# Weight blocks in groups of two, first decay rows by products, and a planned lock between VectorE and POOL

## The chip, the core and the metric

The kernel runs on one core of a Trainium2 chip. A core has five engines that run their own instruction streams and meet at semaphores: TensorE (PE in the profile; its weight loads are shown as PEld), VectorE (DVE), ScalarE (ACT), GpSimd (POOL) and SyncE (SP), which here issues the DMAs. The metric is the device time of one execution in microseconds, as the median of several runs.

## The reference

Attention with a forget gate, followed by a two-layer feed-forward net ("MoE" in the names, though there is only one expert). Batch 8, 8 heads, 576 rows, 64 columns per head; the net has 512 inputs and outputs and 2048 hidden columns. The net's two weight matrices come as 64-bit floats.

```python
scores = scale * np.matmul(q, k.transpose(0, 1, 3, 2))
log_f = np.log(np.clip(f, 0.0001, 1.0))
cum = np.cumsum(log_f, axis=-1)
decay = cum[:, :, :, None] - cum[:, :, None, :]
scores = np.where(causal, -1000000000.0, scores + decay)
attn = np.exp(scores - max) / (sum + 1e-09)
out = np.matmul(attn, v)
...
h = x @ w_in
g = np.where(h >= 1, h, np.where(h <= -1, 0.0, (h + 1) ** 2 / 4))
return g @ w_out
```

Here x is the attention's output with the heads side by side: 4608 tokens of 512 columns.

## The kernel before

**Jobs.** The attention is cut into jobs, one for each batch and pair of heads. Batch 0 is cut once more by rows (`CUTS`): jobs 0 to 3 are rows 0 to 255 of its four head pairs, jobs 4 to 7 its rows 256 to 575; job 8 on are whole batches. A job takes its rows in steps of 128 (`r`). For each step `scores` makes the products of q and k in PSUM (L831) and, on POOL, the decay term in SBUF: `sd = ck * nsig + cqs` (L837), then the causal mask (L841). `ck` holds the running sum of the logarithms along the row, the same in all partitions; `cqs` is the same sum for the row itself, one number in each partition. `weights` adds both and takes the row's minimum on DVE (L923), takes the exponential with its row sum on ACT (L927), and the reciprocal on DVE. The first five jobs (`NPE`) turn their probabilities with products on PE against a diagonal (`turn_rows`, L852 and L863), later ones split them into two f16 halves (L941 and L947) and turn them by DMA (L953). `early_values` or `values` multiplies by v; the result is x, in two f16 halves (L902 and L903, or L977 and L978).

**Decay rows.** `decay_sums` computes all running sums on 64 partitions (L442), one for each batch and head, in the tile `early`, and writes them to DRAM as `cum_d` (L445). `load_first_decay` (jobs 0 to 3, L664) and `load_decay` (later jobs, L675) read a row back, spread over 128 partitions.

**Weights.** A weight matrix comes in pieces of 1 MB, two to a block: piece 2i is 256 hidden columns of `w_in`, piece 2i + 1 the same 256 rows of `w_out`. `weight_split` puts an f32 word together from the two 32-bit halves of a double with three DVE instructions of 128x1024 (L495, L498, L501), takes its norm (L505, `from_norms`), and splits it into two f16 halves (L509, and L511 and L512 on POOL or L514 on DVE). There are 16 pieces in 8 blocks. `CONVERT` says how many conversion steps are written into each job's program.

**MoE.** Tokens are taken in chunks of 256, and a unit is one chunk and one block of 256 hidden columns. `moe_front` makes 24 products for h (L1012), the nonlinearity on ACT and DVE (L1021 to L1023), and g in two f16 halves (L1025 and L1026); `moe_back` adds 12 products to the chunk's output in PSUM (L1041). The scale factors come from `moe_scales`, fifteen small DVE instructions on one to eight columns (L579 to L604). The first two chunks run before all blocks are converted: `EARLY` lists their units in groups, and a group's units have their own scales and their own sum in PSUM, which is copied to the output tile (L1058) or added to it (L1054). A group's scales are written once its last block is converted.

**Order.** The code writes one program. Then `plan` sets every engine's order anew: `traced` finds what depends on what and gives every instruction a rank, its place in the program plus a shift from the table `SHIFT`; `Step.cost` estimates its duration; `arranged` plays the program through, always taking what can begin first, by rank where several can. The orders found are pinned by dependencies without semaphores. All DMAs go through SP in that order. Within an engine nothing overtakes.

Of the kernel before, what the change touches and what calls it, by code (L numbers as in the profile page):

```python
# [91 lines left out]
class Step:  # L92


    def __init__(self, k, ins):
# [22 lines left out]
    def cost(self):  # L118
# [13 lines left out]
        if e == "ACT":  # L132
            return 150 + (0.82 if wide and wide[0][0][:2] in ("s_", "ph", "po") else 0.93) * n + 100 * min(len(self.reads) - 1 + len(self.writes) - 1, 3)
# [187 lines left out]
def kernel(  # L321
# [247 lines left out]

    @of_kind  # L570
    def moe_scales(b, first=0, last=NB - 1, early_group=False):
# [5 lines left out]
        w = early_z[:, :, blocks] if early_group else tiny.tile([P, 5, NB], F32, name="z")  # L577
        z.t, z.h, z.u, z.r, z.o = (w[:, i] for i in range(5))
        nc.vector.tensor_scalar(out=z.t, in0=sw[:, 0, blocks], scalar1=sv[:, b:b + 1], scalar2=None, op0=ALU.mult)  # L579
        nc.vector.tensor_scalar(  # L580
# [641 lines left out]
```

## Time and profile before

| what | value |
|---|---|
| median of three runs | 1062.35 us (1059.92 to 1063.02) |
| the profiled execution | 1060.71 us, span in the trace 1058.9 us |
| TensorE's mean granted clock | 0.973 |
| DMA ck<-cum_d, issue to landing | 4.0 us (median), 288 KB |
| DMA place<-in_moe_w_in_dram, issue to landing | 6.9 us (median), 1024 KB |

The profile is that of one execution. The span runs from the first to the last record; the profiled execution's own time is 1.8 us longer. A group of instructions is named by line, engine and operation, with the tiles written and read, the count, then busy time and mean duration in ns, then the idle time of the engine before them and what ended it. In the timeline the columns are start, duration, engine, line, operation and tiles; a bracket holds the idle time before and who ended it. The table by stretches gives the busy time of each engine in a part of the span, the granted clock (1.00 is full speed), the DMA engines' share and GB/s.

### The profile page before, as it was taken

How to read it: one execution, taken by the hardware profiler on the slowest of the kernel's cores; microseconds unless marked ns; L12 is line 12 of the kernel's file. 1: busy time of each engine (PE TensorE's matmuls, PEld its weight loads, DVE VectorE, ACT ScalarE, POOL GpSimd, SP SyncE). 2: the span in 40 equal slices, each digit the busy share in tenths (PEclk: the TensorE clock that was granted, in tenths of full speed). 3: DMA queues.
4: the chain of work that ended last, by engine and by line, in shares of the span. 5: the costliest groups of instructions: out<-in, count | busy, mean ns of one | idle time of the engine just before them, and what ended most of it. 6: DMA issues, size and time to landing. Idle time of an engine off the chain costs nothing.

```text
span 1058.9 us, 24420 instructions
## 1 busy us (share of the span) xinstructions
PE 1003.1 (95%) x8859; PEld 657.7 (62%) x8859; DVE 793.0 (75%) x2095; ACT 786.9 (74%) x1634; POOL 435.4 (41%) x677
## 2 busy tenths in 40 slices
PE   3769888799999999999999999999999999999998
PEld 2546555366666676667666666666666666677665
DVE  5999999999998878977776677887788866322222
ACT  3788888788888878886776688888888877344443
POOL 2887776736443544442332344454445441000000
PEclk9869899889999999999999999999999999999999
DMA  9967669789997777785455476767676654000000
GB/s 298 305 203 206 167 163 194 182 169 187 198 189 184 175 167 151 170 185 128 119 128 131 81 175 144 158 150 160 147 161 143 142 104 95 3 22 19 3 20 20
DMA packets 406041, 152.18 MB, mean 144 GB/s; under 512 B 379680, under 2 KB 382752, under 8 KB 405920
## 3 DMA queue, kind: packets, MB, share of 16 engines
q1 hardware_dynamic: 405920, 150.62, 61.0%
q8 instruction: 69, 1.13, 0.5%
q14 instruction: 52, 0.43, 0.1%
HBM read 75.64 MB, written 9.58 MB: 80 GB/s over the span
## 4 chain that ended last, share of the span: by engine, by line
PE 56%; DMA 0%; DVE 0%; issue 0%; ACT 0%; DVEq 0%
PE ph L1012 25%; PE po L1041 24%; PE s L831 4%; PE s L968 3%; DMA vst<-in_v_dram 0%; DVE pr L947 0%; PE ph L409 0%; DVE u L1023 0%; PE ph L401 0%; DVE x L978 0%; ACT ot L1058 0%; PE ph L397 0%; ACT u L1022 0%; DVE sdr L923 0%; DVE rc L938 0%
## 5 line engine op out<-in xcount | busy, mean ns | idle before, releaser
L1012 PE MATMUL ph<-x,place 128*128 128x256 f16 (+3 forms) x4608 | 413.1, 247 | 1.2 <-DVE u L1023 0.7
L1041 PE MATMUL po<-place,g 128*128 128x512 f16 x1728 | 403.5, 381 | 2.3 <-ACT g L1025 1.0
L1012 PEld LDWEIGHTS <-place 128*128 128x128 f16 x4608 | 353.2, 99 | 61.9 <-issue 21.3
L1041 PEld LDWEIGHTS <-g 128*128 128x128 f16 x1728 | 165.9, 98 | 180.6 <-issue 8.0
L837 POOL TENSOR_SCALAR sdr<-ck,nsig,cqs 128x128 f32<-128x128 f32 (+1 forms) x192 | 150.1, 789 | 269.3 <-DVE pr L947 258.1
L1023 DVE SCALAR_TENSOR_TENSOR u<-ph,z,u 128x512 f32<-128x512 f32 x128 | 95.6, 747 | 128.5 <-ACT u L1022 128.3
L1021 ACT ACTIVATE u<-ph,z 128x512 f32<-128x512 f32 x128 | 98.8, 772 | 117.3 <-PE ph L1012 116.9
L927 ACT ACTIVATE sdr<-sdr,nm 128x384 f32<-128x384 f32 (+1 forms) x248 | 137.3, 555 | 24.7 <-DVE nm L923 22.2
L947 DVE SCALAR_TENSOR_TENSOR pr<-sdr,rc,pr 128x384 f16<-128x384 f32 (+2 forms) x232 | 126.7, 584 | 8.0 <-ACT pr L941 6.6
L1025 ACT ACTIVATE g<-u,z 128x512 f16<-128x512 f32 x128 | 91.8, 717 | 51.7 <-DVE u L1023 50.9
L1026 DVE SCALAR_TENSOR_TENSOR g<-u,z,g 128x512 f16<-128x512 f32 x128 | 98.2, 767 | 41.0 <-ACT g L1025 40.5
L941 ACT ACTIVATE pr<-sdr,rc 128x384 f16<-128x384 f32 (+1 forms) x236 | 118.7, 556 | 7.3 <-issue 2.8
L831 PE MATMUL s<-qkT 64*64 64x512 f16 (+11 forms) x1056 | 111.4, 336 | 6.0 <-DVE nm L923 2.9
L923 DVE CUSTOM_DVE_ANT_0 sdr<-s,sdr,nalpha 128x128 f32<-128x128 f32 (+1 forms) x192 | 99.0, 544 | 13.1 <-PE s L831 7.4
L841 POOL TENSOR_SCALAR_AFFINE_SELECT sdr<-sdr 128x128 f32<-128x128 f32 x248 | 97.7, 414 | 2.3
L837 POOL TENSOR_SCALAR sd<-ck,nsig,cqs 64x576 f32<-64x576 f32 x48 | 51.1, 1064 | 115.1 <-DMA ck<-cum_d 46.7
L1022 ACT ACTIVATE u<-u 128x512 f32<-128x512 f32 x144 | 89.7, 623 | 1.9
L968 PE MATMUL s<-pT,vs 128*64 128x320 f16 (+3 forms) x1098 | 69.8, 279 | 3.2 <-DVE nm L923 3.2
L968 PEld LDWEIGHTS <-vs 128*64 128x64 f16 x1098 | 48.6, 110 | 27.0 <-issue 9.3
L831 PEld LDWEIGHTS <-qkT 64*128 64x128 f16 (+1 forms) x864 | 32.4, 98 | 44.0 <-issue 29.4
L747 DVE SCALAR_TENSOR_TENSOR qs<-qk,sc,qs 128x640 f16<-128x640 f32 x48 | 45.6, 962 | 5.3 <-ACT qs L745 4.4
L837 POOL TENSOR_SCALAR sdr<-ck,cq 128x384 f32<-128x384 f32 (+3 forms) x48 | 40.4, 842 | 17.1 <-DVE pr L947 12.6
(157 smaller groups left out, 1027.7 us busy)
## 6 DMA issues: line engine op xcount, KB each, us to landing
ck<-cum_d SPq DMA_DIRECT2D x64, 288.0 KB, 4.0
out_dram<-ot SPq DMA_DIRECT2D x36, 256.0 KB, 2.2
qk<-in_k_dram SPq DMA_DIRECT2D x68, 128.0 KB, 2.7
vst<-in_v_dram SPq DMA_DIRECT2D x28, 288.0 KB, 3.4
v<-in_v_dram SPq DMA_DIRECT2D x62, 128.0 KB, 2.8
qk<-in_q_dram SPq DMA_DIRECT2D x60, 128.0 KB, 2.9
place<-in_moe_w_in_dram SPq DMA_DIRECT2D x6, 1024.0 KB, 6.9
place<-in_moe_w_out_dram SPq DMA_DIRECT2D x5, 1024.0 KB, 7.8
```

Of the source, the lines that this page charges most:

```text
L831: nc.tensor.matmul(sds[h % len(sds)][1][p0:p1, c0:c1], lhsT=a[rows, q0 - w.s0:q0 - w.s0 + p1 - p0], rhs=b[rows, c0:c1], start=(i == 0), st ...
L837: nc.gpsimd.tensor_scalar(out=sd[p0:p1, 0:wid], in0=w.ck[h][p0:p1, 0:wid], scalar1=w.nsig if w.p < NQK else w.nsig[p0:p1], scalar2=w.cqs[p ...
L841: nc.gpsimd.affine_select(sd[p0:p1, q0:wid], sd[p0:p1, q0:wid], pattern=[[-1, wid - q0]], channel_multiplier=1, base=0, compare_op=ALU.is_ ...
L923: nc.vector.tensor_tensor_reduce(out=a, in0=sp[:, 0:wid], in1=a, scale=w.nalpha, scalar=BIG, op0=ALU.add, op1=ALU.min, accum_out=nm[:, i:i ...
L927: nc.scalar.activation(a, a, AF.Exp, bias=nm[:, i:i + 1], scale=-1.0, accum_out=sm[:, i:i + 1])
L941: nc.scalar.activation(pr[:, :, 0, i, :], a, AF.Copy, scale=rc[:, i:i + 1])
L947: nc.vector.scalar_tensor_tensor(out=pr[:, :, 1, i, :], in0=a, scalar=rc[:, i:i + 1], in1=pr[:, :, 0, i, :], op0=ALU.mult, op1=ALU.subtract,)
L968: nc.tensor.matmul(av[64 * h:64 * h + 64, at + s0:at + s1], lhsT=w.vs[:, vl, h, t, :], rhs=w.pT[:, t, pl, h, s0:s1], start=(t == 0 and pi ...
L1012: nc.tensor.matmul(ph[:, fi, a0:a1], lhsT=wi[fb][:, wl, t, fi * P:(fi + 1) * P], rhs=xs[b][:, t, xl, s0:s0 + a1 - a0], start=(fi == 0 and ...
L1021: nc.scalar.activation(u, h, AF.Relu, scale=z.u[:, i:i + 1], bias=z.h[:, i:i + 1])
L1026: nc.vector.scalar_tensor_tensor(out=g[:, 1], in0=u, scalar=z.r[:, i:i + 1], in1=g[:, 0], op0=ALU.mult, op1=ALU.subtract)
L1041: nc.tensor.matmul(po[ch][i], lhsT=g[:, gl, fi * TC + i * P:fi * TC + (i + 1) * P], rhs=wo[fb][:, wl, fi, :], start=(first and fi == 0 and ...
```

## The change

**Groups.** `EARLY` gets more and smaller groups, and chunk 1 fewer and larger ones. `FIRST = {4: 2}` puts the values of job 3 in front of job 4's first step, and lets two MoE units follow as soon as they are ready. `CONVERT` has one conversion step in each of jobs 0 to 3 (before: none in job 0, two in job 3). `moe_scales` computes the part that belongs to a block (`block_scales`) once only, for blocks that have none yet, since groups now overlap; each group keeps `r` and `osc` of its own.

**Decay rows of jobs 0 and 1** (`NROW = 2`). Instead of reading back `cum_d`, POOL spreads a column of the identity over 128 columns (`picks`), and PE multiplies it with the running sums: each partition of the product is the picked row. It stands in PSUM, in a tile named `po1`, and as POOL doesn't read PSUM here, ACT makes `sd` of it with one activation (scale `nsig`, bias `cqs`). The mask stays on POOL. Jobs 2 and 3 are as before.

**The plan.** `arranged` gets a lock: a DVE instruction that counts as sharing (a `TensorScalarPtr` or `TensorTensor` of more than one column whose first operand isn't one of the PSUM tiles) and any POOL instruction exclude each other. The later of the two is taken to begin near the other's end, and an instruction that would have to wait is passed over for one that can begin sooner. The cost estimates of DVE, ACT and POOL get new constants, and `SHIFT` other entries.

```diff
+NROW = 2
-EARLY = ((0, 0, 4), (0, 4, 6), (1, 0, 4), (1, 4, 6), (0, 6, 8), (1, 6, 8))
-
-CONVERT = {1: 1, 2: 1, 3: 2, 5: 1, 6: 1, 9: 1, 10: 2}
+EARLY = ((0, 0, 2), (0, 2, 4), (0, 4, 6), (1, 0, 6), (0, 6, 8), (1, 6, 8))
+FIRST = {4: 2}
+
+CONVERT = {0: 1, 1: 1, 2: 1, 3: 1, 5: 1, 6: 1, 9: 1, 10: 2}
...
-SLOW = 1.03
+SLOW = 1.02
+AWARE = True
 LOOK = 50
 SHIFT = {
+    ("across", "DVE"): -800,
+    ("decay_sums", "SP"): -100,
+    ("first_values", "SP"): 200,
+    ("from_norms", "DVE"): -800,
     ("from_norms", "PE"): -100,
-    ("measure", "DVE"): 400,
-    ("moe_back", "DVE"): 200,
-    ("moe_back", "SP"): 800,
+    ("join_scales", "DVE"): 200,
+    ("moe_back", "DVE"): -100,
+    ("moe_front", "DVE"): 400,
+    ("prepare", "ACT"): 1500,
+    ("prepare", "DVE"): -800,
     ("split_values", "ACT"): 1500,
-    ("turn_rows", "ACT"): -25,
-    ("value_max", "DVE"): -100,
-    ("weight_split", "DVE"): 200,
-    ("weights", "POOL"): 400,
+    ("values", "DVE"): 25,
+    ("weights", "POOL"): 200,
 }
...
+        self.shares = (
+            self.engine == "DVE" and ins.opcode in ("TensorScalarPtr", "TensorTensor")
+            and self.writes[0][4] > 1 and self.reads[0][0][:2] not in ("s_", "ph", "po")
+        )
...
         if e == "POOL":
             if self.ins.opcode == "TensorTensor":
-                return 450 + 2.0 * n
-            return 260 + 0.95 * n if "Affine" in self.ins.opcode else 460 + 1.15 * n
+                return 185 + 1.89 * n
+            return 177 + 0.86 * n if "Affine" in self.ins.opcode else 322 + 0.83 * n
...
-        return 170 + 55 * (scalars > 0) + (0.6 if fast else 1.08) * n + (20 if len(self.writes) > 1 else 0)
+        return 147 + 62 * (scalars > 0) + (0.52 if fast else 1.04) * n
...
                     begin = max(t, free[e])
+                    if AWARE and s.shares:
+                        begin = max(begin, pool - 140)
+                    elif AWARE and e == "POOL":
+                        begin = max(begin, hold - 100)
...
             end = t + s.time
+            if e == "POOL":
+                if hold > t:
+                    end = max(end, hold + s.time - 100)
+                pool = end
+            elif s.shares:
+                if pool > t:
+                    end = max(end, pool + max(s.time - 140, 24))
+                hold = end
             free[e] = end - OVERLAP[e]
...
+        if early_group:
+            at = groups.index((first, last + 1))
+            z.t, z.h, z.u = (early_z[:, i * NB + first:i * NB + first + n] for i in range(3))
+            z.r = early_r[:, starts[at]:starts[at] + n]
+            z.osc = early_r[:, starts[-1] + at:starts[-1] + at + 1]
+            fresh = slice(made[0], last + 1)
+            if made[0] <= last:
+                block_scales(*(early_z[:, i * NB + made[0]:i * NB + last + 1] for i in range(3)), b, fresh)
+                made[0] = last + 1
...
     def load_first_decay(w):
         bh = w.b * H + 2 * w.hp
+        if w.p < NROW:
+            pt = ps1.tile([P, DM], F32, name="po1").rearrange("p (h s) -> p h s", h=2)
+            for h in range(2):
+                nc.gpsimd.tensor_copy(picks[h], ident[0:B * H, bh + h:bh + h + 1].broadcast_to([B * H, P]))
+                nc.tensor.matmul(
+                    pt[:, h], lhsT=picks[h], rhs=early[0:B * H, 2 * S:2 * S + w.s1], start=True, stop=True
+                )
+            w.ck += [pt[:, 0], pt[:, 1]]
+            picks[0:2] = []
+            return
...
-            nc.gpsimd.tensor_scalar(
-                out=sd[p0:p1, 0:wid], in0=w.ck[h][p0:p1, 0:wid], scalar1=w.nsig if w.p < NQK else w.nsig[p0:p1],
-                scalar2=w.cqs[p0:p1, r, h:h + 1], op0=ALU.mult, op1=ALU.add,
-            )
+            if w.p < NROW:
+                nc.scalar.activation(
+                    sd[:, 0:wid], w.ck[h][:, 0:wid], AF.Identity, scale=w.nsig, bias=w.cqs[:, r, h:h + 1]
+                )
+            else:
+                nc.gpsimd.tensor_scalar(
+                    out=sd[p0:p1, 0:wid], in0=w.ck[h][p0:p1, 0:wid], scalar1=w.nsig if w.p < NQK else w.nsig[p0:p1],
+                    scalar2=w.cqs[p0:p1, r, h:h + 1], op0=ALU.mult, op1=ALU.add,
+                )
...
-            steps.insert(4 if len(steps) == NT5 else 2, finish)
+            steps.insert(0 if p in FIRST else 4 if len(steps) == NT5 else 2, finish)
...
-        quota = -(-ready() // (NPAIR - (p + NPAIR - 1) % NPAIR))
+        quota = FIRST.get(p) or -(-ready() // (NPAIR - (p + NPAIR - 1) % NPAIR))
```

`picks` are four slices of a tile of the ring named `u`, 64 partitions by 128 columns each. `block_scales` holds the six instructions of `moe_scales` that stood at L579 to L588.

More of the change, by code (lines that the diff above doesn't have):

```diff
@@ L132, in cost @@
         if e == "ACT":
[L133 removed]
+            return 190 + 0.845 * n + 92 * min(len(self.reads) - 1 + len(self.writes) - 1, 3)
         if e == "POOL":
             if self.ins.opcode == "TensorTensor":
[L136 to L137 removed]
+                return 185 + 1.89 * n
+            return 177 + 0.86 * n if "Affine" in self.ins.opcode else 322 + 0.83 * n
         if wide:
@@ L226, in arranged @@
     chains = {e: [] for e in LATE}
+    hold = pool = 0
     fly, dma, warm, border, busy, form = [], 0.0, False, WINDOW, 0.0, None
@@ L457, in decay_sums @@
         )
+    picks = two.tile([P, 2 * TC], F32, name="u")
+    picks = [picks[0:B * H, P * i:P * i + P] for i in range(2 * NROW)]
     place = const.tile([P, 2 * NB + 1, 2, 2 * DM], F16, name="place")
@@ L563, in value_scale, with block_scales @@
         scale_of(sv[:, b:b + 1], pv[:, b:b + 1], m)
-    early_z = const.tile([P, 5, NB], F32, name="early_z")
+    groups = sorted({e[1:] for e in EARLY})
+    starts = [sum(e - f for f, e in groups[:i]) for i in range(len(groups) + 1)]
+    early_z = const.tile([P, 3 * NB + starts[-1] + len(groups)], F32, name="early_z")
+    early_r = early_z[:, 3 * NB:]
+    made = [0]
     class Scales:
         pass
+    def block_scales(t, h, u, b, blocks):
+        nc.vector.tensor_scalar(out=t, in0=sw[:, 0, blocks], scalar1=sv[:, b:b + 1], scalar2=None, op0=ALU.mult)
+        nc.vector.tensor_scalar(
+            out=h.bitcast(I32), in0=t.bitcast(I32), scalar1=1, scalar2=None, op0=ALU.logical_shift_right
+        )
+        nc.vector.tensor_scalar(
+            out=h.bitcast(I32), in0=h.bitcast(I32), scalar1=HALF_BIAS, scalar2=None, op0=ALU.add
+        )
+        nc.vector.reciprocal(u, h)
+        nc.vector.tensor_scalar(out=u, in0=u, scalar1=0.5, scalar2=None, op0=ALU.mult)
+        nc.vector.tensor_scalar(out=h, in0=h, scalar1=0.5, scalar2=None, op0=ALU.mult)
     @of_kind
@@ L576, in moe_scales @@
         n = last + 1 - first
[L577 to L580, printed above, removed]
-            out=z.h.bitcast(I32), in0=z.t.bitcast(I32), scalar1=1, scalar2=None, op0=ALU.logical_shift_right
-        )
-        nc.vector.tensor_scalar(
-            out=z.h.bitcast(I32), in0=z.h.bitcast(I32), scalar1=HALF_BIAS, scalar2=None, op0=ALU.add
-        )
-        nc.vector.reciprocal(z.u, z.h)
-        nc.vector.tensor_scalar(out=z.u, in0=z.u, scalar1=0.5, scalar2=None, op0=ALU.mult)
-        nc.vector.tensor_scalar(out=z.h, in0=z.h, scalar1=0.5, scalar2=None, op0=ALU.mult)
+        if early_group:
[8 more added lines that the diff above has]
+        else:
+            w = tiny.tile([P, 5, NB], F32, name="z")
+            z.t, z.h, z.u, z.r = (w[:, i] for i in range(4))
+            z.osc = w[:, 4, 0:1]
+            block_scales(z.t, z.h, z.u, b, blocks)
         gm = tiny.tile([P, 1], F32, name="gm", bufs=2)
@@ L1072 @@
     units += [(ch, fb) for ch in range(NCH) if ch not in [e[0] for e in EARLY] for fb in range(NB)]
-    groups = sorted({e[1:] for e in EARLY})
     done = 0
@@ L1180 @@
                 converted += 1
-            while ready() and done - before < quota * (i + 1) // len(steps):
+            while ready() and done - before < (quota if p in FIRST else quota * (i + 1) // len(steps)):
                 if units[done] not in bsc and nw < 2 * NB:
```

5 lines of the change are left out of this document (3 added, 2 removed).

## The prediction

> **What bounds the kernel now.** I read the page's first part first, then the same busy times cut into stretches, then the waits of TensorE in the first 100 us, then the instructions around them in order of time.
>
> ```profile
> PE 1003.1 (95%) x8859; PEld 657.7 (62%) x8859; DVE 793.0 (75%) x2095; ACT 786.9 (74%) x1634; POOL 435.4 (41%) x677
> ```
> ```profile
> 0.00:9.00 9.00, 1.97 (x16) 1.60 (x16) 3.17 (x4) 2.56 (x3) 2.45 (x13) 1.00 0.73 218
> 9.00:23.00 14.00, 7.17 (x40) 4.83 (x40) 9.95 (x22) 2.81 (x4) 2.43 (x5) 1.00 0.98 324
> 23.00:54.00 31.00, 20.38 (x128) 15.06 (x128) 26.89 (x72) 23.80 (x68) 25.45 (x36) 0.83 0.99 316
> 54.00:86.00 32.00, 22.53 (x98) 15.00 (x98) 29.34 (x61) 25.39 (x52) 27.57 (x26) 0.68 0.73 232
> 86.00:110.00 24.00, 23.66 (x184) 14.56 (x183) 23.54 (x50) 21.72 (x41) 17.56 (x20) 1.00 0.64 155
> 110.00:231.00 121.00, 103.84 (x718) 59.81 (x719) 114.52 (x322) 102.67 (x216) 82.30 (x111) 0.90 0.77 177
> 231.00:1059.00 828.00, 823.52 (x7680) 546.82 (x7678) 585.59 (x1570) 608.00 (x1254) 277.67 (x468) 1.00 0.57 125
> ```
>
> Each row has the stretch, its length, the busy time of PE, PEld, DVE, ACT and POOL, the granted clock, the DMA share and GB/s. After 231 us PE is idle for 828 - 823.52 = 4.5 us and has the full clock: there PE is the bound, and a faster DVE, ACT or POOL gives at most those 4.5 us. Before 231 us PE is busy 1.97 + 7.17 + 20.38 + 22.53 + 23.66 + 103.84 = 179.6 us, so it idles 51.4 us; and busy time times what the clock lacks (20.38 x 0.17 + 22.53 x 0.32 + 103.84 x 0.10) is another 21 us at a lower clock, an estimate from these means. **The front, 0 to 231 us, holds all that can be won.** Who ends the waits there? DVE is busy 71% from 9 to 23, 87% from 23 to 54, 92% from 54 to 86, 98% and 95% after. From about 54 us on DVE is the bound of the front: it carries attention, MoE and the conversion of the weights at once. Before that there is a gap with another cause:
>
> ```profile
> PE ph L863 <- ACT pr L852: 22.7, 8, 9.5
> ```
> ```profile
> 12.12 2.73 SPq L664 DMA_DIRECT2D ot<-cum_d  x3
> 15.48 0.69 DVE L495 TENSOR_SCALAR qs<-place 128x1024 int32<-128x1024 int32 x1 [1.42 <-DMA place<-in_moe_w_in_dram]
> 20.31 1.92 POOL L837 TENSOR_SCALAR sdr<-ot,cq 128x128 f32<-128x128 f32 x2 [17.24 <-DMA ot<-cum_d]
> 22.63 0.29 DVE L923 CUSTOM_DVE_ANT_0 sdr<-s,sdr 128x128 f32<-128x128 f32 x1 [0.63 <-POOL sdr L841]
> 25.47 0.17 DVE L930 TENSOR_SCALAR rc<-sm 128x2 f32<-128x2 f32 x1 [2.30 <-ACT sdr L927]
> 26.39 1.22 PE L863 MATMUL ph<-pr,sdr 128*128 128x128 f32 x4 [9.47 <-ACT pr L852]
> ```
>
> The chain of the first job is to be read here: the decay rows go out to DRAM and back (issued from 12.12), POOL can use them at 20.31, DVE's row minimum follows at 22.63, PE's first turning of probabilities at 26.39. One of PE's eight waits for L852 is that one, 9.5 us.
>
> **The change, part by part.** First, the decay rows of jobs 0 and 1. Removed: two DMAs of 256 KB out of four (their share of the SP queue too), and half of POOL's decay instructions of jobs 0 to 3. Added: four copies on POOL, four products on PE, eight activations on ACT.
>
> ```profile
> L837 POOL TENSOR_SCALAR sdr<-ot,cq 128x128 f32<-128x128 f32 (+1 forms) x8 | 7.5, 942 | 17.9 <-DMA ot<-cum_d 17.2
> L837 POOL TENSOR_SCALAR pr<-ot,cq 128x128 f32<-128x128 f32 (+1 forms) x8 | 5.3, 668 | 1.2 <-ACT sdr L927 0.5
> L927 ACT ACTIVATE sdr<-sdr,nm 128x128 f32<-128x128 f32 x4 | 1.6, 398 | 0.4 <-DVE nm L923 0.4
> L863 PE MATMUL ph<-pr,sdr 128*128 128x128 f32 x24 | 6.2, 424 | 15.2 <-ACT pr L852 15.2
> L923 DVE CUSTOM_DVE_ANT_0 sdr<-s,sdr 128x256 f32<-128x256 f32 x12 | 4.8, 409 | 0.0
> L923 DVE CUSTOM_DVE_ANT_0 sdr<-s,sdr 128x128 f32<-128x128 f32 x12 | 3.2, 285 | 1.4 <-PE s L831 0.8 <-POOL sdr L841 0.6
> ```
>
> POOL loses (7.5 + 5.3) / 2 = 6.4 us of work in the stretch where it is busy 25.45 of 31 us. The four products have 256 columns where the nearest row, L863, has 128, so 4 x 2 x 0.424 = 3.4 us of PE between 9 and 23, where PE is idle for 6.8 us: nothing. Should that cover go, they cost their 3.4 us. ACT's eight cost about 8 x 0.45 = 3.6 us (0.40 for 128 columns, some 0.1 more for 256) between 9 and 23, where ACT is busy 2.81 of 14 us: nothing there, and 3.6 us if they land after 23. The four copies on POOL are not in the trace; POOL sits idle 17.24 us before 20.31, which hides anything up to that.
>
> The running sums exist when the DMA out is issued, at 9 us; two products, two activations, POOL's mask and DVE's minimum can then follow by about 13 us instead of 22.63. What is late next: the weights, which come at 15.48 in any case, and DVE. So the gain isn't those 9 us but only what DVE can do in its holes. From 9 to 54 DVE is idle 4.05 + 4.11 = 8.2 us. What becomes ready for them is the DVE work of jobs 0 and 1, per job 2 x 0.285 + 2 x 0.409 = 1.4 us of minima and about as much of small scalings and the split of x, together 5.6 us. I take **-4.5 us**; bounds: 0, if the weights set the pace (the DMA share is 0.98 and 0.99 here, so DMA is nearly full), and -8.2, all holes filled. The two DMAs removed are 0.5 MB at 324 GB/s, 1.6 us earlier for the weights behind them; that lies inside these bounds.
>
> Second, groups of two blocks. The first unit can begin with two blocks converted instead of four.
>
> ```profile
> 68.97 0.14 DVE L591 TENSOR_REDUCE gm<-mp 128x1 f32<-128x4 f32 x1
> 71.85 2.26 DVE L603 TENSOR_SCALAR early_z<-early_z 128x4 f32<-128x4 f32 x1
> 74.14 0.18 DVE L604 RECIPROCAL early_z<-early_z 128x4 f32<-128x4 f32 x1
> 75.47 0.47 DVE L903 SCALAR_TENSOR_TENSOR x<-po,sv,x 128x256 f16<-128x256 f32 x1
> ```
> ```profile
> L1012 PE MATMUL ph<-x,place x528: 192/272/421, 85.7 to 263.0; 128*128 128x256 f16 x128, 128*128 128x64 f16 x24, 128*128 128x192 f16 x24
> ```
>
> The group's scales are done at 74.3, x of chunk 0 at 75.9, and PE begins MoE at 85.7. So the scales of four blocks were not late before x: what a smaller group can gain is that its scales and splits leave the DVE queue in front of x. It gains PE work for a stretch (54 to 86) in which PE idles 9.5 us and has a clock of 0.68. But DVE is the bound there, and a unit brings DVE work along. I take **-2.5 us**; bounds 0 and -7.2 (22.53 x 0.32, if the clock is full there). It costs scales: five groups instead of three. A group has nine instructions of its own and six for new blocks, which fall due four times instead of three: 2 x 9 + 6 = 24 more on DVE, at 0.14 us (the row of L591) **+3.4 us**. Upper bound: the fifteen instructions from 68.97 to 74.32 took 5.35 us, so 24 / 15 x 5.35 = 8.6 us; lower: 24 x 0.1 = 2.4, since neighbours overlap. The sums into the output tile stay equal in number: chunk 0 adds three times and chunk 1 once, before it was twice and twice. The conversion moved one job earlier meets weights that land when they land, so I put it at nothing.
>
> Third, the lock. Some DVE instructions last far longer than their like in the same trace, and the longest lie under a POOL instruction:
>
> ```profile
> 71.95 2.12 POOL L512 TENSOR_TENSOR place<-place 128x1024 f16<-128x1024 f32 x1
> ```
> ```profile
> L603 DVE TENSOR_SCALAR early_z<-early_z x3: 222/229/2257, 71.8 to 219.1; 128x2 f32<-128x2 f32 x2, 128x4 f32<-128x4 f32 x1
> L1026 DVE SCALAR_TENSOR_TENSOR g<-u,early_z,g 128x512 f16<-128x512 f32 x16 | 17.6, 1098 | 0.3 <-ACT g L1025 0.2
> L1026 DVE SCALAR_TENSOR_TENSOR g<-u,z,g 128x512 f16<-128x512 f32 x98 | 75.6, 771 | 18.1 <-ACT g L1025 17.6
> L935 DVE TENSOR_SCALAR rc<-sm 128x2 f32<-128x2 f32 x29 | 8.1, 280 | 1.5 <-ACT sdr L927 1.5
> L935 DVE TENSOR_SCALAR rc<-sm 128x2 f32<-128x2 f32 x89 | 16.3, 183 | 11.9 <-ACT sdr L927 11.4
> L514 DVE SCALAR_TENSOR_TENSOR place<-place,sw 128x1024 f16<-128x1024 f32 x5 | 8.1, 1611 | 0.8 <-ACT place L509 0.8
> L514 DVE SCALAR_TENSOR_TENSOR place<-x,sw,place 128x1024 f16<-128x1024 f32 x3 | 3.8, 1265 | 0.0
> ```
>
> L603 on 128x4 took 2.26 us, from 71.85 to 74.11, and POOL's L512 ran from 71.95 to 74.07; its like took 0.22. In the front (first row of each pair) against later or unhurt ones: 16 x (1.098 - 0.771) = 5.2 us, 29 x (0.280 - 0.183) = 2.8, 5 x (1.611 - 1.265) = 1.7, and 2.0 for that one L603: 11.7 us of DVE time in four groups, most of it where DVE is the bound. A plan that sees the lock can put a minimum (it reads PSUM, and its 285 and 409 ns rows show no such tail) under a POOL instruction. It can't do so always, since DVE is over 90% busy with mostly instructions of the hurt kind, so I take under half: **-5 us**. Bounds: -11.7, and +4 where the plan holds back an engine that then idles (a third of the same sum, in the other direction).
>
> The Trainium skill, page "SBUF — State Buffer", section "Who interferes with whom", says that two SBUF inputs, or a two-port mode, on DVE contend with GpSimd, and that "Issue order, not op shape, decides who blocks." The L603 row agrees. That last sentence speaks against this part: a plan fixes the order on each engine and not the moment of issue between two engines; by it this term would be 0 and the sum -3.6 us.
>
> The new constants and the shifted ranks reorder everything; no row prices them. After 231 us they can win 4.5 us at most; I put them at 0.
>
> **Sum:** -4.5 - 2.5 + 3.4 - 5 = -8.6 us. Against the profiled execution (1060.7 us, span 1058.9) that is 1052.1; the median of the three runs, 1062.35, lies 1.6 us above it, so the forecast is 1053.8 us.
>
> **The rivals.** (a) **More comes off.** DVE's holes all fill (-8.2), the lock falls by two thirds (-8), the clock of 54 to 86 recovers mostly (-5), scales +3.4: -17.8, 1044.6 us. For it: PE waits 22.7 us for L852 alone before 100 us. Against: DVE is busy 92% and more from 54 us on, and all this must pass through it.
>
> (b) **Nothing comes of it.** The weights set the pace before 54 us, so the earlier decay rows turn into a wait for weights (-1.6, the DMA time removed); the run's own issue order undoes the planned lock (0); an earlier first unit (-2) pays for its scales (+3.4): 0, 1062 us. For it: a DMA share of 0.98 to 0.99 from 9 to 54. This is also the case that the change doesn't do what it says. The Trainium skill's sentence on issue order, above, would make this case.
>
> (c) **Slower: the early units get ahead of the conversion.** Two units of chunk 0 are due in job 4's first step, with their scales; on DVE they come before the conversion of blocks 4 to 7 and the minima of the long rows.
>
> ```profile
> L1023 DVE SCALAR_TENSOR_TENSOR u<-ph,early_z,u 128x512 f32<-128x512 f32 x16 | 11.9, 741 | 1.3 <-ACT u L1022 1.3
> ```
>
> Price: 2 x (0.741 + 1.098) = 3.7 us of units that come too early, scales at their hurt price 8.6, less 4.5 and 1.6 from the decay rows: +6 us, 1068.5 us. It decides from the moment that DVE has no hole left (54 us on), and only if the last conversion ends later than now. For it: DVE's 92 to 98%. Against: PE's idle 9.5 us there, which the same units fill, and a unit gives PE 12 + 24 matmuls for two DVE instructions.
>
> **How the numbers follow.** A measurement of this kernel tells a change of about 0.3%, 3.2 us. Forecast 0.42 (1047 to 1059), (a) 0.20 (1037 to 1047), (b) 0.17 (1059 to 1065.5), (c) 0.21 (1065.5 to 1072). Faster: 0.42 + 0.20 = 0.62; same 0.17; slower 0.21. The range 1040 to 1068 leaves out the outer third of (a) and about half of (c), under 0.2 together; the bounds of the unknown terms (0 to -8.2, 0 to -7.2, +2.4 to +8.6, +4 to -11.7) reach somewhat farther than that only if all end on one side. The forecast's own range is 1047 to 1059.
>
> **What would show it.** Decay rows: the first L923 (row minimum) before 15 us, PE's first probability turning before 19, and DVE busier than 9.95 of 14 us from 9 to 23. Groups: MoE's first matmul well before 85.7, a granted clock above 0.68 between 54 and 86, five groups of scales. Lock: L1026 in the front near 0.8 us instead of 1.10, L935 near 0.2. Sum: PE idle before its steady part some 43 us instead of 51.4, with no new idle time after. I am wrong if DVE's busy time in the front stays as it is with the lock's tails in other groups, if the last group's scales come later than now, or if PE gets gaps after 231 us, where it has 4.5 us of them today.

## The result, and the profile after

| | before | after |
|---|---|---|
| median | 1061.68 us (1059.92 to 1063.02, four runs) | 1076.18 us (1073.85 to 1080.60, four runs) |
| ratio | | **1.0147** [1.0131, 1.0164] |
| the profiled execution | 1060.71 us, span 1058.9 | 1080.60 us, span 1078.8 |

The change makes the kernel 14.5 us slower; 8 us less was forecast, and the time lies outside the range. The profiled execution of after is its longest of four, 4.4 us above the median, so its stretches hold a little more than the difference of the medians. In the table of experiments the median of before on two of the chips still contains one slow run, which makes the differences there 0.15 (c1, c2, e4, e5) and 0.3 us (a40, a60, p40, p75) smaller; the ratios leave it out.

The page's first part, and then the table by stretches of after (columns as in the prediction):

```profile
PE 1016.5 (94%) x8867; PEld 668.6 (62%) x8867; DVE 770.4 (71%) x2119; ACT 794.7 (74%) x1642; POOL 419.8 (39%) x673
```
```profile
0.00:9.00 9.00, 4.79 (x30) 4.00 (x32) 3.90 (x6) 2.63 (x4) 3.62 (x17) 1.00 0.73 228
9.00:23.00 14.00, 12.20 (x49) 7.98 (x47) 8.74 (x29) 10.02 (x28) 2.64 (x8) 1.00 1.06 383
23.00:54.00 31.00, 20.11 (x106) 15.14 (x107) 27.43 (x79) 22.15 (x51) 22.98 (x24) 0.79 0.78 224
54.00:86.00 32.00, 27.62 (x151) 18.60 (x150) 24.23 (x56) 24.33 (x50) 20.82 (x23) 0.77 0.94 277
86.00:110.00 24.00, 14.96 (x102) 9.11 (x104) 20.79 (x48) 19.43 (x40) 16.70 (x21) 0.92 0.62 138
110.00:231.00 121.00, 101.69 (x680) 58.81 (x678) 108.54 (x325) 96.70 (x204) 74.36 (x106) 0.89 0.80 178
231.00:1079.00 848.00, 835.11 (x7761) 554.98 (x7761) 576.79 (x1582) 619.41 (x1269) 278.67 (x476) 1.00 0.60 122
```

Read it against the same table of before. Up to 86 us PE is busy 64.7 us where it was 52.1: the early gain is there. It is lost again at once: from 86 to 110 PE falls from 23.66 to 14.96. Over the whole front, 0 to 231 us, PE is busy 181.4 us (before 179.6), but 4.3 us of that are the new products (below), so the front has done no more for the rest than before; of the records of MoE's two product lines (L1071 and L1100, before L1012 and L1041) it holds 444 where it held 463. After 231 us there are 20 us more (848 against 828): 11.6 us more of busy PE (work left over by the front, and some 3 us, by estimate, of a lower clock: 0.99 from 265 to 600 us, where before has 1.00), and idle time up from 4.5 to 12.9 us.

DVE is the opposite of what its share suggests. Its busy time in the front fell from 207.4 to 193.6 us, by 13.8 us, and its idle time rose by the same amount. What it waits for now, by the view of waits of DVE, 0 to 231 us (total, times, longest):

```profile
DVE sdr L982 <- PE s L885: 12.7, 5, 4.0
DVE m L570 <- DMA vst<-in_v_dram: 5.0, 5, 1.7
...
DVE pr L982 <- PE s L885: 3.2, 2, 2.9
```

and in before, same view:

```profile
DVE sdr L923 <- PE s L831: 1.9, 4, 0.9
...
DVE m L544 <- DMA vst<-in_v_dram: 0.4, 1, 0.4
```

**The freed DVE time became DVE waiting for PE and for a DMA.** PE, in turn, waits for DVE. The waits of PE over the whole of after:

```profile
PE s L885 <- DVE nm L982: 12.5, 9, 4.3
PE s L768 <- DVE x L1037: 7.5, 2, 4.6
PE ph L433 <- ACT pT L933: 6.3, 1, 6.3
PE ph L433 <- ACT place L531: 6.0, 3, 4.2
...
PE ph L922 <- ACT pr L911: 1.9, 2, 1.6
```

The 22.7 us for L852 in before (L911 is its line in after) are down to 1.9; others stand in their place. I read this, two engines that wait for each other in turn with neither busy, as an order that does not fit. One such place can be followed in the timeline of after, on SP, DVE and PE:

```profile
255.62 0.43 SPq L563 DMA_DIRECT2D vst<-in_v_dram  x1
```
```profile
258.49 0.08 DVE L982 DVE_READ_ACCUMULATOR2_ANT nm<- 128x1 f32 x1
262.66 0.75 DVE L570 TENSOR_REDUCE m<-vst 128x1 f32<-128x576 f32 x1 [4.09 <-DMA vst<-in_v_dram]
263.33 0.88 DVE L849 SCALAR_TENSOR_TENSOR vs<-v,sv,vs 128x640 f16<-128x640 f32 x1
264.13 0.48 DVE L982 CUSTOM_DVE_ANT_0 sdr<-s,sdr,nalpha 128x256 f32<-128x256 f32 x1
...
266.73 0.08 DVE L982 DVE_READ_ACCUMULATOR2_ANT nm<- 128x1 f32 x1
```
```profile
266.86 0.61 PE L885 MATMUL s<-qkT 64*128 64x512 f16 x2 [4.29 <-DVE nm L982]
```

L570 takes the maximum of a later batch's values. The plan put it at the head of DVE's queue at 258.5 us, but its data had been asked for only at 255.62 and came at 262.6. Two row minima (L982, at 264.13 and 266.32) stood behind it in DVE's queue; the second was done at 266.8, and for it PE waited 4.29 us, in the stretch where PE is the bound. That is about half of the 8.4 us of new PE gaps after 231 us.

### The profile page after: what moved, and what is told of

Same layout as the page of the kernel before. It is cut to its first block, busy times and chain, and to the rows that moved or that the text cites. A ratio compares the mean times of both kernels' runs of the same rounds, so it can differ in the third digit from the quotient of the medians.

```text
span 1078.8 us, 24463 instructions
## 1 busy us (share of the span) xinstructions
PE 1016.5 (94%) x8867; PEld 668.6 (62%) x8867; DVE 770.4 (71%) x2119; ACT 794.7 (74%) x1642; POOL 419.8 (39%) x673
## 4 chain that ended last, share of the span: by engine, by line
PE 66%; DVE 6%; DMA 3%; SPq 3%; issue 2%; ACT 1%; POOL 0%; DVEq 0%; POOLq 0%
PE ph L1071 28%; PE po L1100 28%; PE s L885 5%; PE s L1027 4%; DMA vst<-in_v_dram 3%; DVE sdr L982 1%; DVE pr L1006 1%; SPq L696 1%; DVE qs L801 1%; SPq L841 1%; SPq L700 0%; DVE m L570 0%; DVE g L1085 0%; SPq L806 0%; DMA ck<-cum_d 0%
## 5 line engine op out<-in xcount | busy, mean ns | idle before, releaser
L1071 PE MATMUL ph<-x,place 128*128 128x256 f16 (+3 forms) x4608 | 412.1, 247 | 0.0
L1100 PE MATMUL po<-place,g 128*128 128x512 f16 x1728 | 404.9, 382 | 3.4 <-DVE g L1085 3.0
L1071 PEld LDWEIGHTS <-place 128*128 128x128 f16 x4608 | 354.3, 99 | 61.4 <-issue 20.2
L1100 PEld LDWEIGHTS <-g 128*128 128x128 f16 x1728 | 167.2, 99 | 180.2 <-issue 7.3
L896 POOL TENSOR_SCALAR sdr<-ck,nsig,cqs 128x128 f32<-128x128 f32 (+1 forms) x192 | 139.8, 732 | 250.4 <-DVE pr L1006 216.7
L1006 DVE SCALAR_TENSOR_TENSOR pr<-sdr,rc,pr 128x384 f16<-128x384 f32 (+2 forms) x232 | 131.2, 590 | 25.4 <-ACT pr L1000 24.0
L885 PE MATMUL s<-qkT 64*64 64x512 f16 (+11 forms) x1056 | 116.3, 334 | 16.2 <-DVE nm L982 12.5
L1085 DVE SCALAR_TENSOR_TENSOR g<-u,z,g 128x512 f16<-128x512 f32 x128 | 96.8, 757 | 36.1 <-ACT g L1084 35.8
L900 POOL TENSOR_SCALAR_AFFINE_SELECT sdr<-sdr 128x128 f32<-128x128 f32 x248 | 106.2, 440 | 14.1 <-ACT sdr L892 5.2
L982 DVE CUSTOM_DVE_ANT_0 sdr<-s,sdr,nalpha 128x128 f32<-128x128 f32 (+1 forms) x192 | 98.5, 544 | 16.3 <-PE s L885 12.6
L896 POOL TENSOR_SCALAR sd<-ck,nsig,cqs 64x576 f32<-64x576 f32 x48 | 48.1, 1002 | 138.4 <-DMA ck<-cum_d 45.4
L1027 PE MATMUL s<-pT,vs 128*64 128x320 f16 (+3 forms) x1098 | 72.4, 286 | 5.4 <-DMA qk<-in_k_dram 3.5
L1027 PEld LDWEIGHTS <-vs 128*64 128x64 f16 x1098 | 51.2, 113 | 28.8 <-issue 9.3
L986 ACT ACTIVATION_READ_ACCUMULATOR sdr<-sdr,nm 128x1 f32 x248 | 46.5, 188 | 0.0
```

What stands on the lines that cost most here:

```text
L885: nc.tensor.matmul(sds[h % len(sds)][1][p0:p1, c0:c1], lhsT=a[rows, q0 - w.s0:q0 - w.s0 + p1 - p0], rhs=b[rows, c0:c1], start=(i == 0), st ...
L896: nc.gpsimd.tensor_scalar(out=sd[p0:p1, 0:wid], in0=w.ck[h][p0:p1, 0:wid], scalar1=w.nsig if w.p < NQK else w.nsig[p0:p1], scalar2=w.cqs[p ...
L900: nc.gpsimd.affine_select(sd[p0:p1, q0:wid], sd[p0:p1, q0:wid], pattern=[[-1, wid - q0]], channel_multiplier=1, base=0, compare_op=ALU.is_ ...
L982: nc.vector.tensor_tensor_reduce(out=a, in0=sp[:, 0:wid], in1=a, scale=w.nalpha, scalar=BIG, op0=ALU.add, op1=ALU.min, accum_out=nm[:, i:i ...
L986: nc.scalar.activation(a, a, AF.Exp, bias=nm[:, i:i + 1], scale=-1.0, accum_out=sm[:, i:i + 1])
L1006: nc.vector.scalar_tensor_tensor(out=pr[:, :, 1, i, :], in0=a, scalar=rc[:, i:i + 1], in1=pr[:, :, 0, i, :], op0=ALU.mult, op1=ALU.subtract,)
```

## The experiments

Three theories. **PLAN**: the new constants, shifts and lock make a worse order. **UNITS**: rival (c), early units and their scales push back the conversion. **RESHUFFLE**: any new order costs some us, whatever the change does, because before's order fits better than those near it. The change splits into three parts: groups (`EARLY`, `FIRST`, `CONVERT`), decay rows (`NROW`) and plan (lock, constants, `SHIFT`). "Last scales" is the start of the last group's reciprocal in the profile, a mark for the end of the conversion; it is 220.9 us in before and 227.3 in after. Differences are to the median of before on the same chip.

| run | what it is | median, us | ratio to before | us | last scales |
|---|---|---|---|---|---|
| e1_old_plan | groups + rows, before's plan | 1068.74 | 1.0080 [1.0064, 1.0097] | +8.7 | 229.8 |
| e2_new_plan_only | before + new plan | 1077.94 | 1.0170 [1.0155, 1.0185] | +17.9 | 226.0 |
| e3_rows_only | before + rows | 1071.72 | 1.0109 [1.0094, 1.0124] | +11.7 | 225.6 |
| e4_groups_only | before + groups | 1080.11 | 1.0185 [1.0168, 1.0202] | +19.1 | 231.5 |
| e5_old_shift | after, `SHIFT` of before | 1084.98 | 1.0225 [1.0209, 1.0242] | +23.9 | 238.5 |
| e6_no_lock | after without the lock | 1101.49 | 1.0391 [1.0373, 1.0409] | +41.4 | 240.1 |
| c1_look60 | before, `LOOK` 60 | 1068.76 | 1.0073 [1.0054, 1.0091] | +7.7 | 222.4 |
| c2_look40 | before, `LOOK` 40 | 1068.49 | 1.0073 [1.0057, 1.0089] | +7.4 | 226.3 |
| a40_after_look | after, `LOOK` 40 | 1088.51 | 1.0248 [1.0220, 1.0275] | +28.0 | 235.7 |
| a60_after_look | after, `LOOK` 60 | 1085.82 | 1.0231 [1.0208, 1.0254] | +25.3 | 231.7 |
| e2b_look60 | e2, `LOOK` 60 | 1072.89 | 1.0120 [1.0101, 1.0138] | +12.2 | 225.0 |
| p40_rows_kept | rows, first 40 us planned anew | 1060.16 | 1.0008 [0.9993, 1.0023] | -0.3 | 220.6 |
| p75_rows_kept | rows, first 75 us planned anew | 1065.16 | 1.0044 [1.0027, 1.0061] | +4.7 | 224.9 |
| d1_delay_conversion | before's order, DVE work added in front | 1064.56 | 1.0036 [1.0021, 1.0051] | +3.7 | 224.9 |
| d2_delay_later | before's order, DVE work added later | 1063.22 | 1.0023 [1.0014, 1.0033] | +2.4 | 219.3 |
| l1_no_pool_split | before's order, less POOL work | 1054.40 | 0.9942 [0.9923, 0.9960] | -6.3 | 214.5 |
| g1_first_off | after, `FIRST` empty | 1082.05 | 1.0203 [1.0188, 1.0218] | +21.2 | 232.4 |
| g2_convert_early | after, last conversions earlier | 1089.24 | 1.0272 [1.0254, 1.0289] | +28.4 | 206.7 |

**The parts by themselves.** e1 takes the plan back, e2 takes the other two parts back, e3 and e4 leave one of those two under before's plan, e6 takes the lock alone out of after.

For e1, e3 and e4, from after (with before's constants and `SHIFT`; e3 also has before's `EARLY` and `CONVERT` and no `FIRST`, e4 also `NROW = 0`; e2 has these two edits without the plan's):

```diff
-SLOW = 1.02
-AWARE = True
+SLOW = 1.03
+AWARE = False
```

For e1, e3, e4 and e6 the lock's effect on the ends goes with it; e6 has this and `AWARE` alone:

```diff
-            if e == "POOL":
+            if not AWARE:
+                pass
+            elif e == "POOL":
                 if hold > t:
```

> The changed kernel with the plan of before (no lock, old constants, old rank shifts); groups of two and decay rows by products stay. Theory PLAN (the new order on the engines costs the 14.5 us): back to the time of before or under it, 1052 to 1062 us. Theory UNITS (the early units and their scales get ahead of the conversion): stays slow, 1070 to 1078 us. Theory RESHUFFLE (any new order of this plan lands somewhere, whatever its cause): anything from 1055 to 1080, not explained by either part.

> The kernel before with the new plan alone (lock, constants, rank shifts); groups and decay rows as before. PLAN: slow, 1070 to 1080 us, with PE gaps after 231 us. UNITS: 1052 to 1062 us. RESHUFFLE: anything from 1055 to 1080.

> The kernel before with the decay rows of jobs 0 and 1 by products alone, old plan. PLAN and UNITS both: 1054 to 1060 us, first row minimum before 15 us. RESHUFFLE: 1055 to 1075, the earlier first minimum notwithstanding.

> The kernel before with the groups of two, the early values and one conversion per job alone; old plan, decay rows from DRAM. UNITS (early units and their scales get ahead of the conversion): 1066 to 1072 us, MoE's first matmul before 80 us and the last early group's scales later than 221 us. RESHUFFLE (the order of before is the best of its neighbours, whatever is changed): also 1063 to 1075, but without a later last conversion. If groups are good in themselves, as e1 against e3 suggests (3 us less): 1055 to 1060.

> The changed kernel with the lock alone left out of the plan; new constants and shifts stay. PLAN, if the lock is the part that costs: 1055 to 1066 us. PLAN, if constants or shifts cost: no better, 1072 to 1085, since the new constants without the lock underestimate POOL. UNITS: 1070 to 1080.

Measured: every one of them is slower than before, and they do not add. Rows cost 11.7 us and groups 19.1, both together only 8.7, under the same plan. The plan alone costs 17.9, and with rows and groups on top 14.5. Numbers like these cannot be prices of the parts. Something that is drawn anew in each of these kernels is as large as the parts themselves: for RESHUFFLE, against a clean UNITS (which asks the cost of e1 and e4 to be alike) and against PLAN as the only cause (which asks e1 to be free). Not all fell as expected: e4 and e6 are slower than every range given for them, and e4's last scales are late (231.5 us), as UNITS asks.

**A plan drawn anew without any change of work.** `LOOK` is the time within which the planner holds two instructions to begin alike and takes the one of lower rank. A change of it alters only orders.

```diff
-LOOK = 50
+LOOK = 60
```

> A control: the kernel before with LOOK at 60 instead of 50, the margin in ns within which the plan takes an instruction as ready. No work is added, removed or made earlier. RESHUFFLE: 3 to 15 us slower, 1063 to 1075. Theories that put the loss in a part of the change: within 3 us of before.

> The same control in the other direction, LOOK at 40. RESHUFFLE: 1063 to 1075, not in mirror image of LOOK 60. Otherwise within 3 us of before.

The same instructions, the same tiles, and 7.7 and 7.4 us more. The waits of PE from 86 to 300 us in c1:

```profile
PE s L968 <- DVE nm L923: 6.6, 2, 5.8
PE ph L409 <- ACT qs L728: 4.1, 3, 1.8
```

where before has

```profile
PE s L968 <- DVE nm L923: 3.2, 2, 1.7
...
PE ph L409 <- ACT qs L728: 1.4, 1, 1.4
```

RESHUFFLE is shown for before: two orders next to its own cost 0.7% each. The same for after, and for the plan alone:

> The changed kernel with LOOK at 40: a neighbour of its plan, with no other work. If the changed kernel's order, too, is the best of its neighbours: 1080 to 1092 us. If it is an ordinary draw: 1066 to 1086, on either side of 1076. If a part of the change costs by its work: within 3 us of 1076.

> The changed kernel with LOOK at 60; the same three answers as for LOOK 40: 1080 to 1092, 1066 to 1086 or within 3 us of 1076.

> The kernel before with the new plan alone, and LOOK at 60. If the new plan gives slower orders in general: 1074 to 1092 us, the old plan's neighbours being at 1068.6. If e2 was a bad draw: 1060 to 1072.

Measured against before, after's neighbours lose 10.8 and 13.5 us more than after: it, too, stands lower than the orders beside it. Why before and after lie below their neighbours is not shown; tables of shifts that were chosen by measured time would do it, but how they were chosen is not on record. e2 and e2b have before's work (the same number of instructions on PE, DVE, ACT and POOL) and lose 17.9 and 12.2 us: a changed order alone can cost as much as the whole change. e2b lies 6 us under e2 and 4 to 5 us over c1, between what the theories expected, and does not decide whether the new plan costs something beyond a redraw. Likewise e5, with before's shifts under the new constants and the lock:

> The changed kernel with the rank shifts of before; lock, constants, groups and rows stay. If the new shifts are what the new plan needs: slower than the changed kernel's 1076, 1080 to 1095. If the new shifts are the part that costs: 1060 to 1070. RESHUFFLE: anything from 1065 to 1095.

It is slower still, by 9 us. Nothing speaks for the new shifts as the fault, but 9 us is what a redraw alone can give, so this run doesn't settle it.

**The rows in an order that is kept.** Here only the first part of the program is planned; from there on each engine's instructions stand word for word in before's order.

```diff
-    chains = arranged(*traced(nc, rings, kinds), rings)
+    steps, users, order = traced(nc, rings, kinds)
...
+    only = [s for s in steps if s.kept < FREE]
+    chains = arranged(steps, users, order, rings, only)
+    for s in sorted((s for s in steps if s.kept >= FREE), key=lambda s: s.kept):
+        chains[s.engine].append(s)
```

> Decay rows of jobs 0 and 1 by products, old plan, but only what the plan of before begins in its first 40 us is planned anew; everything behind keeps the order of before word for word (its pick numbers are stored in the kernel). RESHUFFLE: the loss of e3 (11.6 us) goes and the gain of the earlier chain shows, 1052 to 1059 us. If the decay rows cost in themselves (the products, ACT's new work): 1064 to 1072, as e3.

> The same with the first 75 us planned anew. RESHUFFLE, if the loss of e3 arises behind 75 us: 1050 to 1059 us; if it arises between 40 and 75 us: 1062 to 1072. If the decay rows cost in themselves: 1064 to 1072.

The work of e3, p75 and p40 is the same. With all of the order drawn anew it costs 11.7 us, with 75 us of it 4.7, with 40 us nothing that can be measured (interval -0.7 to +2.4 us, and not the gain that RESHUFFLE expected). In p40, by the timeline and the instructions of the scales,

```profile
18.56 0.29 DVE L993 CUSTOM_DVE_ANT_0 sdr<-s,sdr 128x128 f32<-128x128 f32 x1 [0.36 <-PE s L896]
...
21.39 0.78 PE L933 MATMUL ph<-pr,sdr 128*128 128x128 f32 x4 [2.01 <-ACT pr L922]
```
```profile
L659 DVE RECIPROCAL early_z<-early_z x3: 142/160/178, 70.1 to 220.6; 128x2 f32<-128x2 f32 x2, 128x4 f32<-128x4 f32 x1
```

the first minimum comes 4 us earlier (before 22.63) and the first turning 5 us (before 26.39), and the last scales come when they came before. So the decay rows by themselves are worth nothing that can be measured here: the start of the chain moves, the end of the conversion doesn't.

**Is it the late conversion?** In after the last scales come 6.4 us later, as rival (c) wants. g1 takes away the early units in job 4, g2 moves the conversion steps of jobs 9 and 10 one job ahead.

```diff
-FIRST = {4: 2}
+FIRST = {}
```
```diff
-CONVERT = {0: 1, 1: 1, 2: 1, 3: 1, 5: 1, 6: 1, 9: 1, 10: 2}
+CONVERT = {0: 1, 1: 1, 2: 1, 3: 1, 5: 1, 6: 1, 8: 1, 9: 2}
```

> The changed kernel without the early values and units of job 4 (FIRST empty); groups, rows and the new plan stay. UNITS (they get ahead of the conversion): last early scales before 225 us and 1062 to 1070. If the units don't bring the lateness: no better than the changed kernel, 1076 to 1090.

> The changed kernel with the last three conversion steps one job earlier (jobs 8, 9 and 9 instead of 9, 10 and 10). If the end of the conversion sets the time: last early scales near 210 us and 1058 to 1068. If a reordered neighbour is always worse: 1080 to 1092, whatever the conversion does.

g1 is slower than after and its last scales come later, at 232.4: the early units do not hold the conversion up. g2 has its scales earliest of all runs,

```profile
L648 DVE RECIPROCAL early_z<-early_z x5: 155/166/191, 51.1 to 206.7; 128x2 f32<-128x2 f32 x4, 128x6 f32<-128x6 f32 x1
```

14 us before those of before, and is still 28.4 us slower; c1 loses 7.7 us with its last scales only 1.5 us late. **The late scales often go with the loss, but the loss comes without them too**, so as the only cause UNITS falls. g1 and g2 are orders drawn anew as well, so a share of UNITS is not ruled out. To price a delay of the conversion cleanly, d1 keeps before's order and lets DVE do two of the three instructions of one weight piece (L495 and L498) twice more; d2 adds about the same DVE time to job 20, after the front.

```diff
+            for _ in range(2 if n == 14 else 0):
+                nc.vector.tensor_scalar(
+                    out=bits, in0=top, scalar1=0x07FFFFFF, scalar2=3, op0=ALU.bitwise_and, op1=ALU.logical_shift_left
+                )
+                nc.vector.scalar_tensor_tensor(
+                    out=bits, in0=low, scalar=29, in1=bits, op0=ALU.logical_shift_right, op1=ALU.bitwise_or
+                )
```
```diff
-        for j in range(2):
+        for j in (0, 0, 0, 1, 1, 1) if w.p == 20 else (0, 1):
```

> The kernel before, its order kept word for word, with 3.8 us more on DVE just before the last two pieces of weights are converted (the first two instructions of the conversion of piece 14 done three times; the output is the same). If a later end of the conversion is the cause: the last early scales at about 225 us and 2.5 to 5 us slower, 1063 to 1066. If it is only a mark: within 1.5 us of before.

> The same 3.8 us on DVE, order kept, but in job 20, in the steady part where PE is the bound (the split of q and k done three times). Under every theory in which PE is the bound there: within 1.5 us of before. If any DVE delay anywhere passes to the end: 1063 to 1066.

d1: last scales 4.0 us later, end 3.7 us later. d2: end 2.4 us later with the conversion where it was (four more instructions of some 0.89 us, about 3.5 us). The intervals overlap, so the two places are not told apart. What they do show is that in an order that is kept, most of an added DVE microsecond reaches the end, even behind the front, where PE is busy all but 4.5 us and a theory with PE as the bound expected at most 1.5 us.

**The lock in an order that is kept.** l1 has before's order; POOL's two instructions for the low half of `w_in` (L511, L512) are one memset.

```diff
-                nc.gpsimd.tensor_scalar(out=word, in0=word, scalar1=s, scalar2=0.0, op0=ALU.mult, op1=ALU.add)
-                nc.gpsimd.tensor_tensor(out=lo, in0=word, in1=hi, op=ALU.subtract)
+                nc.gpsimd.memset(lo, 0.0)
```

> The kernel before, order kept word for word; POOL's two instructions of 128x1024 for the low half of each w_in piece (L511 and L512, about 4 us for each of eight blocks) are replaced by one memset to zero, so the low half of w_in is left out of the result. If DVE time freed from the lock reaches the end (the step of the prediction): 5 to 10 us faster, 1051 to 1056. If it turns into waits for other engines in a fixed order: within 3 us of before.

6.3 us faster. The groups of l1, 0 to 265 us (L1033, L942 and L521 are L1026, L935 and L514 of before):

```profile
L1033 DVE SCALAR_TENSOR_TENSOR g<-u,early_z,g 128x512 f16<-128x512 f32 x16 | 13.0, 812 | 0.2
...
L519 POOL MEMSET place<- 128x1024 f16 x8 | 7.6, 951 | 4.0 <-ACT place L513 3.9
...
L521 DVE SCALAR_TENSOR_TENSOR place<-place,sw 128x1024 f16<-128x1024 f32 x5 | 6.4, 1284 | 0.0
...
L942 DVE TENSOR_SCALAR rc<-sm 128x2 f32<-128x2 f32 x30 | 5.9, 196 | 2.0 <-ACT sdr L934 1.9
```

The three DVE groups lose their tails: 16 x 0.286 + 30 x 0.084 + 5 x 0.327 = 8.7 us, of which 6.3 reach the end. POOL also has 23.8 us less to do (its four groups of L511 and L512 took 31.4 us), so not all of the gain need be DVE's; POOL was not tried alone. Products with a low half of zeros could also bring a higher granted clock: l1's four runs have 0.981 to 0.985, before on the same chip 0.975 to 0.982. The clock alone doesn't give the gain, since on another chip a run of before at 0.984 took 1061.06 us.

## Why the prediction was wrong, point by point

**The step that failed** is the one sentence "The new constants and the shifted ranks reorder everything; no row prices them. After 231 us they can win 4.5 us at most; I put them at 0." It bounded what a new order can win and gave no bound for what it can lose. No row of before gives one: all of its idle time after 231 us was 4.5 us, and a new order made 12.9 of it. The fourteen kernels whose whole order was planned anew, after among them, are all slower than before, by 7.4 us (no change of work) to 41.4 us. The forecast's other terms, -8.6 us, are hardly larger than the cost of either redraw without any change of work (c1 +7.7, c2 +7.4), and the new plan without any change of work (e2) costs 17.9 us. Two of the forecast's three signs of being wrong came: the last scales, and PE's gaps after 231 us. PE's idle time before 231 us fell to 49.6 us and not to 43.

**Decay rows, -4.5.** The marks came true and the price didn't. Rows of after:

```profile
10.78 0.28 DVE L982 CUSTOM_DVE_ANT_0 sdr<-s,sdr 128x128 f32<-128x128 f32 x1
...
16.12 1.22 PE L922 MATMUL ph<-pr,sdr 128*128 128x128 f32 x4
...
42.52 0.59 PE L433 MATMUL ph<-m2w,ones 128*128 128x2 f32 x2 [6.30 <-ACT pT L933]
```

The minimum is 12 us earlier and the turning 10, but DVE is busy 8.74 us from 9 to 23, not more than 9.95, and from 9 to 54 it idles 8.8 us (before 8.2): its holes did not fill. At 42.52 PE stands 6.3 us for an activation. Kept in before's order the rows give 0 (p40), the end of the interval that I had tied to the weights; what set it there I have not shown.

**Groups, -2.5 and +3.4.** MoE begins at 66.25 us instead of 85.7, and the granted clock from 54 to 86 is 0.77 instead of 0.68, as forecast; then 86 to 110 gives the work back. The extra scales were not tried alone. The 24 instructions are there (2119 on DVE against 2095), and the rows of the early groups, added up, hold about 2 us more than in before, where one L603 alone has 2.0 us of tail.

**Lock, -5.** The forecast's two marks (L1026 near 0.8 us, L935 near 0.2) hold in after; the split L514 is no faster (0 to 265 us; L1085, L994 and L540 are L1026, L935 and L514):

```profile
L1085 DVE SCALAR_TENSOR_TENSOR g<-u,early_z,g 128x512 f16<-128x512 f32 x15 | 11.3, 756 | 0.0
...
L540 DVE SCALAR_TENSOR_TENSOR place<-place,sw 128x1024 f16<-128x1024 f32 x5 | 8.0, 1595 | 1.2 <-ACT place L535 1.2
...
L540 DVE SCALAR_TENSOR_TENSOR place<-x,sw,place 128x1024 f16<-128x1024 f32 x3 | 5.9, 1979 | 0.1
...
L994 DVE TENSOR_SCALAR rc<-sm 128x2 f32<-128x2 f32 x26 | 4.2, 165 | 1.8 <-ACT sdr L986 1.7
```

But they were no marks of the lock. The first of these groups is at 835 ns in c1, whose plan knows no lock, and at 818 in e6; here are the groups of c1 and then those of e6 (after without the lock):

```profile
L1026 DVE SCALAR_TENSOR_TENSOR g<-u,early_z,g 128x512 f16<-128x512 f32 x16 | 13.4, 835 | 0.4 <-ACT g L1025 0.4
```
```profile
L1087 DVE SCALAR_TENSOR_TENSOR g<-u,early_z,g 128x512 f16<-128x512 f32 x14 | 11.4, 818 | 0.6 <-ACT g L1086 0.5
...
L542 DVE SCALAR_TENSOR_TENSOR place<-place,sw 128x1024 f16<-128x1024 f32 x5 | 10.0, 2007 | 0.9 <-ACT place L537 0.9
...
L542 DVE SCALAR_TENSOR_TENSOR place<-x,sw,place 128x1024 f16<-128x1024 f32 x3 | 7.4, 2474 | 0.0
...
L996 DVE TENSOR_SCALAR rc<-sm 128x2 f32<-128x2 f32 x24 | 4.6, 190 | 1.0 <-ACT sdr L988 0.7
```

Before has 1098 ns, and the other orders without a lock have 818 to 939. Like against like, after against e6, the lock takes 15 x 0.062 + 5 x 0.412 + 3 x 0.495 + 26 x 0.025 = 5.1 us off these groups: the size of the term was right, by DVE time, as far as one pair of profiles can tell. One profile is not much: d2, whose front has before's order, has 962 ns in the first group and 1989 in the split's first, where before has 1098 and 1611. Over all runs the first group is at 818 to 1098 ns in the seven orders planned without the lock (before, c1, c2, e1, e3, e4, e6) and at 748 to 834 in the eight with it (after, e2, e2b, e5, a40, a60, g1, g2): lower, with a small overlap. The Trainium skill, "SBUF — State Buffer", "Who interferes with whom", has issue order decide who blocks, from which the prediction read 0 for this term. Both sides show in after, on DVE and POOL (L538 is before's L512):

```profile
47.52 1.28 DVE L540 SCALAR_TENSOR_TENSOR place<-place,sw 128x1024 f16<-128x1024 f32 x1 [0.83 <-ACT place L535]
47.76 3.03 POOL L538 TENSOR_TENSOR place<-place 128x1024 f16<-128x1024 f32 x1
```
```profile
72.22 2.13 POOL L538 TENSOR_TENSOR place<-place 128x1024 f16<-128x1024 f32 x1
72.35 3.08 DVE L540 SCALAR_TENSOR_TENSOR place<-x,sw,place 128x1024 f16<-128x1024 f32 x1
```

In each pair the one that begins first takes its short time and the other is held. At 72 us the plan missed by 0.13 us. One split of after begins within 0.6 us behind the start of such a POOL instruction, three of e6 do (3.0 to 3.1 us each): here the plan made the case rarer and did not rule it out. At the end after is 27 us faster than e6, far more than 5.1, so most of that is again the order. That DVE time counts at all is right in an order that is kept (l1, d1); in the new one the 13.8 us that DVE was busy less became waits.

**"DVE is the bound of the front"** was too coarse. A busy share of 92 to 98% held stretched instructions, which l1 shortens, and it said nothing of whether the next instruction in DVE's queue would find its data once DVE had time. In after it often didn't.

**The rivals.** (c) had the sign, and its condition, a later last conversion, came true; its cause found no support in g1 and g2, and its price was +6 where 14.5 came. (b) named the run's own issue order as what could undo the lock's plan, and saw no loss in it. I had no rival "the new order by itself is worse", which is what c1 and c2 show to exist.

**What stays open.** How the 14.5 us divide between a redraw and a fault of the new plan. For a fault speaks that the new plan is above the old in each like pair: 17.9 against 0, 12.2 against 7.7 (`LOOK` 60), 14.5 against 8.7 (with groups and rows). Against it speaks that the differences, 4.5 to 17.9 us, are hardly larger than the 5.7 to 13.5 us between neighbours of one plan. Groups and plan were not tried in an order that is kept. The place at 258 us shows one flaw (a value maximum ahead of its DMA); whether a better plan for it would bring back its 4.3 us was not tried. No kernel that does all of the work was faster than before by more than can be measured.

## What to carry to other kernels

Where queues are in order and a planner writes them, a change of any constant is a change of the whole order; first time a few plans that alter the order and nothing else, and hold a change worth less than their spread (here 7 to 8 us of 1061) for something that one plan can't show. To learn what a part is worth, keep the order of everything else word for word and change the part alone. A mark that should show one mechanism is worth something only if a control without that mechanism lacks it.

## What the runs showed of the hardware

The tails of DVE under POOL depend strongly on what POOL runs: with a memset of 128x1024 f16 (951 ns) in the place of two instructions with a sum of some 3.9 us (31.4 us for eight pairs), DVE's 128x1024 split took 1284 ns where it had taken 1611, and 128x512 g took 812 where it had taken 1098. The Trainium skill, "SBUF — State Buffer", "Who interferes with whom", says that a DVE instruction with two SBUF inputs contends with a GpSimd instruction that reads SBUF and not with one that only writes it; the memset only writes, and these rows agree. The memset is also shorter, but l1's timeline tells the two apart:

```profile
39.99 1.23 DVE L509 SCALAR_TENSOR_TENSOR place<-place,qs 128x1024 int32<-128x1024 int32 x1
40.05 0.95 POOL L519 MEMSET place<- 128x1024 f16 x1
```
```profile
50.33 0.96 POOL L519 MEMSET place<- 128x1024 f16 x1
...
50.47 0.85 DVE L937 TENSOR_SCALAR rc<-sm 128x2 f32<-128x2 f32 x1
```

The instruction with two SBUF inputs (L509, 1.2 us in the median of this run) and the memset beside it both take their usual time, while a scaling of 128x2 lasts until the memset has ended. So the small scalings, which I had not expected of instructions with two elements in a partition, have tails too: a mean of 280 ns in before (L935) against 196 in l1.

The products with 256 columns in f32 took more than I had worked out: 0.674 us for each record, 4.3 us in all instead of 3.4.

```profile
L710 PE MATMUL po<-x,u 64*128 64x256 f32 x8 | 4.3, 674 | 0.3 <-ACT sdr L892 0.3
```
